# Attention outputs on quarters of the PE array, two tiles a visit, and another order of the opening

## The chip, the cores and the metric

The program runs on one core of a Trainium2 chip. Its engines are PE (TensorE: weight loads and matmuls), ACT (ScalarE), DVE (VectorE), POOL (GpSimd) and SP (SyncE, which issues DMAs here). Each engine takes its own instructions in order and waits on semaphores for the others. The metric is the device time of one execution in microseconds, lower is better.

## What is computed

Three layers follow each other on 4608 tokens of width 512 (8 batches of 576 tokens, 8 heads of 64). The reference, cut:

```python
kv  = einsum('bhsd,bhse->bhde', k, v)            # linear attention, f32
o   = einsum('bhsd,bhde->bhse', q, kv)
rms = sqrt(mean(o * o, axis=-1, keepdims=True) + 1e-06)
x   = (o / rms * g_norm), heads side by side      # (4608, 512)
h   = x @ moe_w_in;  x = (h / (1 + exp(-h))) @ moe_w_out      # d_ff 2048
h   = x @ moe2_w_in; x = (s * relu(h)**2 + b) @ moe2_w_out
```

## The kernel before

**Stages.** The first stage makes seven blocks of 512 tokens of hidden activations with plain products (`emit_h`, 16 groups a block, 112 groups of 12 products `ph`), while the attention of the batches 1 to 7 is worked off between these groups. `hidden1`, `out2`, `hidden3` and `out4` then compute the rest of the two layers with a seven-product scheme for 2x2 blocks. Products of the two layers are three passes over a high and a low part of each operand.

**Attention.** Tokens come in tiles of 128. For a batch, `emit_kv` sums k-transposed times v for the eight heads into one PSUM bank (`pkv`) and copies the eight 64x64 matrices into `kvw`, in which a pair of heads stands as a 128x128 matrix with two blocks on its diagonal and zeros elsewhere; there are two such rooms, for even and odd batches. `emit_qT` transposes a tile of q on PE (`pq`) and copies it on ACT. `emit_out` multiplies it with `kvw`, 4 products of 128x128x128 (`po`); a batch has four tiles and 64 tokens over, and the leftovers of two batches share a fifth tile, with two half products a pair. `emit_squares` and `reduce_sum` give the mean square of each head, `rsqrt_steps` its reciprocal root by twelve DVE operations, `emit_norm` scales the tile (`xnp`), and `emit_xT` transposes it (`px`) and makes the high and low parts `xh` (ACT) and `xl` (DVE) that `ph` reads.

**Order.** The program is in an order written by hand (`manual_schedule`). After each group `ph` of block j, row m, `first_stage` calls `attend(16 * j + m)`. `UNITS` gives for each batch its number of tiles and its first slot; `attend` does what is due at that distance from it: q and kv loads, `emit_kv` two slots ahead, one tile's transposes one slot ahead of its outputs, the root's steps (kept in `between` and run between other DVE work), normalisation, and one tile's `px` a slot. In block 0 `first_stage` also decodes the first layer's weights for later rows: steps `rebias` (ACT), `low`, `sign`, `merge` (DVE), `high` (ACT, the rounded part `wh`), `rest` (DVE, the remainder `wl`).

**Opening.** Batch 0 goes first, alone. Its loads are issued on SP, and on ACT for the leftovers and small columns. `warm_up` keeps PE busy with products that nobody reads. Then come the transposes of q, the kv matrices by pairs of heads, the outputs of the four tiles, squares, root, scaling and `px`; the weights 0 and 1 are decoded beside them.

Of the kernel before, what the change touches and what calls it, by code (L numbers as in the profile page):

```python
# [17 lines left out]
def kernel(  # L18
# [95 lines left out]
    def runs(t):  # L114
        b, c = t
        return [(0, P, b)] if c < TT else [(i * ST, ST, b - 1 + i) for i in range(2)]

# [225 lines left out]
    def emit_kv(b, pairs):  # L343
# [13 lines left out]
        for p, (_, kz, _, vz) in parts:  # L357
            for i, r in enumerate(halves):
                nc.tensor.matmul(ps[r, p, r], kz[i], vz[i], start=False, stop=True, skip_group_check=True)  # L359
        for r in halves:  # L360
            nc.scalar.copy(kvw[b % 2][r, pairs[0]:pairs[-1] + 1, r], ps[r, pairs[0]:pairs[-1] + 1, r])
# [11 lines left out]
    def emit_qT(t):  # L373
        a = q_t.pop(t).rearrange("p h d -> p (h d)")
        ps = ps_a.tile([P, T], F32, tag="a", name=f"pq{t[0]}_{t[1]}")
        for p in range(NP):
            nc.tensor.transpose(ps[:, p * P:(p + 1) * P], a[:, p * P:(p + 1) * P], ident)  # L377
        qT = at_kvw[:, 0].rearrange("p (a t) -> p a t", a=NP)
        nc.scalar.copy(qT.rearrange("p a t -> p (a t)"), ps)
        qT_t[t] = qT  # L380

    def emit_out(t, ps, pairs):

        po = ps.rearrange("p h d -> p (h d)")
# [7 lines left out]
    def emit_squares(t, ps, ms):  # L392

        sq = work.tile([P, H, D], F32, tag="sg", name=f"sq{t[0]}_{t[1]}", bufs=3)
        nc.scalar.activation(sq, ps, AF.Square)
        nc.vector.reduce_sum(ms, sq, axis=AX.X)  # L396

    def rsqrt_steps(r, tiles):
# [10 lines left out]
        for _ in range(3):  # L409
            yield lambda: nc.vector.tensor_mul(a, y, y)  # L410
            yield lambda: nc.vector.scalar_tensor_tensor(a, a, -0.5, ms, op0=ALU.mult, op1=ALU.mult)
            yield lambda: nc.vector.scalar_tensor_tensor(y, a, 1.5, y, op0=ALU.add, op1=ALU.mult)
# [15 lines left out]
    def emit_norm(t, x, y):  # L428
        xn = xn_t.get(t)
        if xn is None:  # L430
            xn = xn_t[t] = xn_page(t)
# [4 lines left out]
    def out_tile(t):  # L436
        b, i = t
        if i == 0:
            r_t[b] = small.tile([P, 4, 6 * H], F32, tag="r", name=f"r{b}", bufs=1)
        ps = ps_a.tile([P, H, D], F32, tag="a", name=f"po{b}_{i}")  # L440
        emit_out(t, ps, range(NP))
        emit_squares(t, ps, r_t[b][:, 0, i * H:(i + 1) * H])
        xn_t[t] = xn_page(t)
        nc.scalar.copy(xn_t[t], ps)
# [98 lines left out]
    def first_qT(t, qs):  # L543
        ps, tag = (ps_a, "a") if t < 2 else (ps_h, "h")
        ps = ps.tile([P, T], F32, tag=tag, name=f"pq{t}")
        for h in range(H):
            r = slice(h % 2 * D, (h % 2 + 1) * D)
            c = slice(h // 2 * P, (h // 2 + 1) * P)
            nc.tensor.matmul(ps[r, c], qs[h // NP][:, h % NP, t, :], ident, start=True, stop=True)
# [3 lines left out]
        nc.scalar.copy(qT, ps)  # L553
# [6 lines left out]
    def attend(slot):  # L560

        for b, n, s in UNITS:
            d = slot - s
            lead = 4 if b == 1 else 8
            if 0 <= d + lead < n:
                load_q(b, d + lead)
            if -1 <= d < NP - 1 and b + 1 < B:
                load_kv(b + 1, d + 1)
        for b, n, s in UNITS:
            d = slot - s  # L570
            if d == -2:
                emit_kv(b, range(NP))
            if 0 <= d < n:
                out_tile((b, d))
            if -1 <= d < n - 1:
                emit_qT((b, d + 1))
# [9 lines left out]
            if TT + 3 <= d < 2 * TT + 3:  # L586
                xT_tile((b, d - TT - 3))
            if n > TT:
                if d == TT + 4:
                    between.extend(rsqrt_steps(r_t[b], [TT]))  # L590
                if TT + 4 <= d < TT + 6:
                    run_between(6)
                if d == TT + 6:
                    norm_tile((b, TT))
                if d == 2 * TT + 3:
                    xT_tile((b, TT))
# [427 lines left out]
    def warm_up(n):  # L1024

        ps = ps_h.tile([P, T], F32, tag="h", name="warm")
        for _ in range(n):
            nc.tensor.matmul(ps, kvw[1][:, 0, :], kvw[1].rearrange("p a t -> p (a t)"), start=True, stop=True)
# [165 lines left out]
    with tc.manual_schedule():  # L1194
# [121 lines left out]
```

## Time and profile before

| | |
|---|---|
| median of 3 runs | 1557.99 us (1557.68 to 1559.7) |
| the profiled execution | 1557.85 us |
| its span, first to last instruction | 1555.7 us |
| busy share of the span | PE 99%, DVE 65%, ACT 53%, POOL 0% |
| granted PE clock, mean | 0.999 |

The rows quoted further down are from this execution, with times from the start of the span. The chain of waits is followed back from the last instruction to what released each; 97% of it is PE. A wait of PE is read from the list of waits; what a stretch costs on PE is read from the start of one piece of the chain to the start of the next. A matmul's record is longer than its slot on the engine, since matmuls overlap; an f32 product leaves two records.

### The profile page before, as it was taken

The page shows a single profiled execution, that of the slowest core. Times are in us where ns is not written, and L with a number is a line of the kernel's source. Part 1 is how long each engine was busy: PE and PEld are TensorE (multiplying, and loading weights), DVE is VectorE, ACT ScalarE, POOL GpSimd, SP SyncE. Part 2 cuts the span into 40 slices and gives each one's busy share as a digit, 9 for nine tenths or more (in the row PEclk, how much of TensorE's full clock was granted, in tenths as well). Part 3 has the DMA queues.
Part 4 walks back from the last instruction along what each step waited for, and adds up shares of the span by engine and source line. Part 5 has one row for each costly group of instructions (what it writes and reads, how often), then busy time and mean ns, then how long its engine had stood idle before and what let it go on. Part 6 is the DMA issues. An engine that isn't in the chain of part 4 may idle for free.

```text
span 1555.7 us, 21812 instructions
## 1 busy us (share of the span) xinstructions
PE 1541.1 (99%) x8184; PEld 1297.8 (83%) x8184; DVE 1017.0 (65%) x1435; ACT 822.4 (53%) x1311; POOL 1.6 (0%) x8
## 2 busy tenths in 40 slices
PE   7999999999999999999999999999999999999999
PEld 5888888888888888888988888888899888888888
DVE  5655466457673968685786666767656767575855
ACT  4655545555465544444545565656555454545554
POOL 0000000000000000000000000000000000000000
PEclk9999999999999999999999999999999999999999
DMA  8988798877665883724669556474577782726242
GB/s 257 302 275 274 265 303 286 293 261 260 254 237 185 349 312 93 242 83 149 217 249 403 210 200 242 176 265 175 200 277 281 292 302 70 243 71 236 87 128 90
DMA packets 228969, 353.77 MB, mean 227 GB/s; under 512 B 56576, under 2 KB 97024, under 8 KB 228864
## 3 DMA queue, kind: packets, MB, share of 16 engines
q1 hardware_dynamic: 163968, 243.83, 46.6%
q10 hardware_dynamic: 64896, 108.55, 18.6%
q8 instruction: 64, 1.05, 0.3%
q14 instruction: 41, 0.34, 0.1%
HBM read 211.81 MB, written 140.51 MB: 226 GB/s over the span
## 4 chain that ended last, share of the span: by engine, by line
PE 97%; DMA 1%; DVE 1%; ACT 0%; issue 0%; SPq 0%; ACTq 0%; DVEq 0%
PE ph L500 19%; PE qy L996 19%; PE qx L996 13%; PE qv L996 13%; PE py L722 12%; PE pv L722 8%; PE px L722 8%; PE po L387 2%; PE px L464 1%; PE pkv L353 1%; PE pt L921 1%; PE pq L377 1%; DMA q<-in_q_dram 1%; DMA kv<-in_v_dram 0%; PE pkv L359 0%; DVE r L396 0%
## 5 line engine op out<-in xcount | busy, mean ns | idle before, releaser
L996 PE MATMUL qy<-o,w 128*128 128x512 f32 (+1 forms) x1440 | 299.1, 368 | 0.0
L996 PEld LDWEIGHTS qy<-o,w 128*128 128x128 f32 x1440 | 251.2, 189 | 45.0
L881 DVE TENSOR_TENSOR o<-ka,o 128x1024 fp32r<-128x1024 f32 (+1 forms) x160 | 178.7, 1117 | 104.8 <-ACT o L879 103.8
L879 ACT CAST o<-ka 128x1024 fp32r<-128x1024 f32 (+1 forms) x160 | 154.6, 968 | 162.9 <-PE qv L996 73.1
L996 PE MATMUL qv<-o,w 128*128 128x512 f32 (+1 forms) x960 | 202.9, 369 | 0.0
L996 PE MATMUL qx<-o,w 128*128 128x512 f32 (+1 forms) x960 | 202.9, 369 | 0.0
L996 PEld LDWEIGHTS qx<-o,w 128*128 128x128 f32 x960 | 167.0, 189 | 29.7 <-DVE o L881 0.2
L996 PEld LDWEIGHTS qv<-o,w 128*128 128x128 f32 x960 | 167.0, 189 | 29.4
L722 PE MATMUL py<-x,w 128*128 128x512 f32 (+1 forms) x720 | 161.2, 368 | 0.0
L722 PEld LDWEIGHTS py<-x,w 128*128 128x128 f32 x720 | 126.5, 189 | 22.7 <-ACT py L777 0.3
L507 ACT ACTIVATE g<-ph 128x512 f32<-128x512 f32 x112 | 67.0, 598 | 145.8 <-PE ph L500 143.5
L500 PE MATMUL ph<-xh,wh 128*128 128x512 f32 x448 | 127.6, 406 | 0.8 <-ACT xh L468 0.8
L879 ACT CAST o<-r 128x1024 fp32r<-128x1024 f32 (+1 forms) x80 | 77.2, 965 | 83.9 <-PE qy L996 43.8
L500 PE MATMUL ph<-xl,wh 128*128 128x512 f32 x448 | 120.4, 390 | 0.0
L500 PE MATMUL ph<-xh,wl 128*128 128x512 f32 x448 | 120.4, 390 | 0.0
L881 DVE TENSOR_TENSOR o<-r,o 128x1024 fp32r<-128x1024 f32 (+1 forms) x80 | 89.4, 1118 | 36.4 <-ACT o L879 35.5
L722 PE MATMUL pv<-x,w 128*128 128x512 f32 (+1 forms) x480 | 111.6, 368 | 0.0
L722 PE MATMUL px<-x,w 128*128 128x512 f32 (+1 forms) x480 | 111.6, 368 | 0.0
L500 PEld LDWEIGHTS ph<-xh,wl 128*128 128x128 f32 x448 | 84.1, 188 | 18.6
L500 PEld LDWEIGHTS ph<-xl,wh 128*128 128x128 f32 x448 | 84.1, 188 | 18.6
L722 PEld LDWEIGHTS px<-x,w 128*128 128x128 f32 x480 | 84.9, 189 | 15.1
L722 PEld LDWEIGHTS pv<-x,w 128*128 128x128 f32 x480 | 84.7, 189 | 14.9
(162 smaller groups left out, 1872.1 us busy)
## 6 DMA issues: line engine op xcount, KB each, us to landing
r<-gt SPq DMA_DIRECT2D x96, 512.0 KB, 4.6
gt<-g ACTq DMA_DIRECT2D x176, 256.0 KB, 2.3
w<-wd SPq DMA_DIRECT2D x84, 512.0 KB, 7.3
gt<-g ACTq DMA_DIRECT2D x56, 512.0 KB, 4.5
wd<-wo SPq DMA_DIRECT2D x112, 256.0 KB, 4.1
wr<-in_moe_w_in_dram SPq DMA_DIRECT2D x16, 1024.0 KB, 6.4
wr<-in_moe_w_out_dram SPq DMA_DIRECT2D x16, 1024.0 KB, 6.5
ka<-gt SPq DMA_DIRECT2D x32, 512.0 KB, 4.0
```

The lines of the kernel that those rows point to most:

```text
L353: nc.tensor.matmul(ps[r, p, r], ka[:, i, d], va[:, i, d], start=(p == pairs[0] and c == 0), stop=False, skip_group_check=True,)
L377: nc.tensor.transpose(ps[:, p * P:(p + 1) * P], a[:, p * P:(p + 1) * P], ident)
L387: nc.tensor.matmul(po[off:off + n, p * P:(p + 1) * P], qT_t[t][:, p, off:off + n], kvw[b % 2][:, p, :], start=True, stop=True,)
L464: nc.tensor.transpose(ps[:, p, :], xn[:, p * P:(p + 1) * P], ident)
L500: nc.tensor.matmul(ps, wt[:, c, :], xt[:, c, :], start=(n == 0 and c == 0), stop=(n == 2 and c == KT - 1))
L507: nc.scalar.activation(both[:, i], ps, AF.Silu)
L722: nc.tensor.matmul(ps, a[s][c], x[t][c], start=(k in (P1, P5) and n == c == 0), stop=(n == 2 and c == 1), skip_group_check=True,)
L879: nc.scalar.copy(o[:, :, 0], x)
L881: nc.vector.tensor_sub(o[:, :, 1], x, o[:, :, 0])
L921: nc.tensor.transpose(ps[:, e * P:(e + 1) * P], self.c[b, h, e][:, r * P:(r + 1) * P], ident)
L996: nc.tensor.matmul(ps, t[:, s], self.o[u][:, i, p], start=(k in (P1, P5) and a == i == m == 0), stop=(a == NA - 1 and i == 1 and m == 2), ...
```

## The change

- `kvw` loses its zeros: for each batch parity, four pairs, two heads on the two halves of the partitions, 64x64 each.
- An output tile is 16 products of 64x64x64. The row half of the array is the head of the pair and picks the PSUM bank, the column half is the half of the tile's tokens. A bank holds the even or the odd heads of two tiles.
- `attend` takes two tiles a visit: transposes of two, outputs of two, then two copies into `xnp` and the squares read from there; `px` of two tiles a visit. The normalisation moves into `norms`, which in block 0 runs ahead of `ph`, in later blocks behind `attend`.
- The root has ten operations with other constants.
- In block 0 `first_weights` decodes one row pair less ahead, and stands before `emit_h`.
- The opening issues q first, then the first weights, k and v, the small columns (now on SP), and the second weights. Its products of q are ordered by halves of the heads, its copies of the kv matrices are on DVE, its squares come in two halves, and the last bank is scaled by eight ACT operations.

The diff, cut:

```diff
-    at_kvw = pair("T", "at_kvw")
-    kvw = [at_kvw[:, 1].rearrange("p (a t) -> p a t", a=NP), const.tile([P, NP, P], F32, tag="kvw1", name="kvw1")]
+    kvw = const.tile([P, 2, NP, D], F32, tag="kvw1", name="kvw")
...
         for r in halves:
-            nc.scalar.copy(kvw[b % 2][r, pairs[0]:pairs[-1] + 1, r], ps[r, pairs[0]:pairs[-1] + 1, r])
+            (nc.scalar.copy if b else nc.vector.tensor_copy)(kvw[r, b % 2, ps_of], ps[r, ps_of, r])
...
+    def emit_qT(b, cs):
+        qT = pair("T", f"qT{b}_{cs[0]}")
+        for n, c in enumerate(cs):
+            a = q_t.pop((b, c)).rearrange("p h d -> p (h d)")
+            ps = bank(f"y{n}_0", f"pq{b}_{c}")
+            for p in range(NP):
+                nc.tensor.transpose(ps[:, p * P:(p + 1) * P], a[:, p * P:(p + 1) * P], ident)
+            nc.scalar.copy(qT[:, n], ps)
...
+    def emit_out(t, banks, pairs):
         for p in pairs:
-            for off, n, b in runs(t):
-                nc.tensor.matmul(
-                    po[off:off + n, p * P:(p + 1) * P], qT_t[t][:, p, off:off + n], kvw[b % 2][:, p, :],
-                    start=True, stop=True,
-                )
+            for i, r in enumerate(ROWS):
+                for c, b in zip(ROWS, sources(t)):
+                    nc.tensor.matmul(
+                        banks[i][c, p, :], qT_t[t][r, p, c], kvw[r, b % 2, p, :], start=True, stop=True
+                    )
...
+    def out_tiles(b, cs):
...
+        for n, c in enumerate(cs):
+            emit_out((b, c), [x[:, n] for x in banks], range(NP))
+            xn_t[b, c] = xn_page((b, c))
...
+        for n in range(2):
+            nc.scalar.copy(x[:, :, :, n], banks[n])
+        for c in cs:
+            emit_squares((b, c), xn_t[b, c], r_t[b][:, 0, c * H:(c + 1) * H])
...
+            if d in (-1, 1, 3):
+                cs = [c for c in (d + 1, d + 2) if c < n]
+                if cs:
+                    emit_qT(b, cs)
+            if d in (0, 2, 4):
+                cs = [c for c in (d, d + 1) if c < n]
+                if cs:
+                    out_tiles(b, cs)
+            if d in (TT + 3, TT + 5):
+                for i in range(2):
+                    xT_tile((b, d - TT - 3 + i))
...
+    def first_weights(m):
+        i = m // 2
+        norms(m)
+        if m % 2 == 0:
+            if i + 1 < NF:
+                decode_first(i + 1, "high", "rest")
+            if i + 2 < NF:
+                decode_first(i + 2, "rebias", "low")
+        elif i + 2 < NF:
+            decode_first(i + 2, "sign", "merge")
+
     def first_stage(j, m, steps):
-        if j == 0:
-            i = m // 2
-            if m % 2 == 0:
-                if i + 2 < NF:
-                    decode_first(i + 2, "high")
-                if i + 3 < NF:
-                    decode_first(i + 3, "rebias", "low")
-            else:
-                if i + 2 < NF:
-                    decode_first(i + 2, "rest")
-                if i + 3 < NF:
-                    decode_first(i + 3, "sign", "merge")
         attend(MT * j + m)
+        if j:
+            norms(MT * j + m)
...
+        qs = [first_load_q(0), first_load_q(1)]
+        kvz = first_load_z()
         load_raw(1, 0, "wr_0")
-        qs = [first_load_q(0), first_load_q(1)]
-        kvs = [first_load_kv(0), first_load_kv(1)]
-        kvz = first_load_z()
+        kvs = [first_load_kv(p) for p in range(NP)]
...
         load_raw(1, 1, "wr_1")
-        kvs += [first_load_kv(2), first_load_kv(3)]
...
         decode_first(0, "rebias", "low", "sign", "merge")
...
+        copy_qT(2)
+        copy_qT(3)
         first_kv(0)
         first_kv(1)
...
+        decode_first(0, "high", "rest")
+        first_out(0)
+        first_kv(2)
+        first_out(1)
+        first_kv(3)
+        first_squares(slice(0, 2))
+        first_out(2)
+        first_out(3)
+        first_squares(slice(2, 4))
+        decode_first(1, "rebias")
...
-        decode_first(1, "rest")
-        decode_first(2, "rebias", "low", "sign", "merge")
+        decode_first(1, "low", "sign", "merge")
...
         for j in range(PB):
             for m in range(MT):
+                if j == 0:
+                    first_weights(m)
                 emit_h(j, m)
                 first_stage(j, m, steps)
```

PE in block 0, from the fourth hidden group's last pass to the first outputs of batch 1. Before:

```order
L500 MATMUL ph_3_542<-xh_402,wl_427 128x512 x4
L377 MATMUL pq_0_570<-ident,qp_66 128x128 x4
L500 MATMUL ph_4_576<-xh_402,wh_451 128x512 x4
L500 MATMUL ph_4_576<-xl_403,wh_451 128x512 x4
L500 MATMUL ph_4_576<-xh_402,wl_470 128x512 x4
L387 MATMUL po_0_603<-kvw_70,at_kvw 128x128 x4
L377 MATMUL pq_1_612<-ident,qp_66 128x128 x4
```

The same place after:

```order
L514 MATMUL ph_3_605<-xh_459,wl_492 128x512 x4
L383 MATMUL pq_0_626<-ident,qp_65 128x128 x4
L383 MATMUL pq_1_632<-ident,qp_65 128x128 x4
L514 MATMUL ph_4_644<-xh_459,wh_532 128x512 x4
L514 MATMUL ph_4_644<-xl_460,wh_532 128x512 x4
L514 MATMUL ph_4_644<-xh_459,wl_534 128x512 x4
L394 MATMUL po_0_0_664<-kvw,qT_0_625 64x64 x2
L394 MATMUL po_0_1_665<-kvw,qT_0_625 64x64 x2
```

The second tile's transposes have moved ahead of the hidden group, and a visit of outputs begins with pairs of 64x64 products (`po_0_0` the even heads' bank, `po_0_1` the odd heads'), sixteen for each of two tiles.

ACT from the last `xh` of batch 0 (the high part of the first block) to the first two Silus `g`. Before:

```order
L468 ACTIVATE xh_402<-px_420,cols 128x4x128
L154 ACTIVATE wr_2_224<-wr_2_224 128x1024
L507 ACTIVATE g_0_449<-ph_0_436 128x512
L173 CAST wh_451<-wf_2_432 128x1024
L154 ACTIVATE wr_3_311<-wr_3_311 128x1024
L507 ACTIVATE g_0_449<-ph_1_456 128x512
```

After:

```order
L482 ACTIVATE xh_459<-px_477,cols 128x4x128
L176 CAST wh_490<-wf_1_486 128x1024
L157 ACTIVATE wr_2_259<-wr_2_259 128x1024
L521 ACTIVATE g_0_509<-ph_0_496 128x512
L521 ACTIVATE g_0_509<-ph_1_517 128x512
```

The rounding of the second weights (`wh` from `wf_1`) stood ahead of all `xh` before; now it stands between the last `xh` and the first Silu.

DVE in the opening, from the first weights' merge (`wf_0`) to the first reduction of squares. Before:

```order
L161 SCALAR_TENSOR_TENSOR wf_0_222<-wr_0_173 128x1024
L176 TENSOR_TENSOR wl_228<-wf_0_222,wh_226 128x1024
L156 TENSOR_SCALAR wr_1_188<-wr_1_188 128x1024
L158 SCALAR_TENSOR_TENSOR wr_1_188<-wr_1_188 128x1024
L161 SCALAR_TENSOR_TENSOR wf_1_309<-wr_1_188 128x1024
L396 TENSOR_REDUCE r_214<-sq_0_362 128x8
```

After:

```order
L164 SCALAR_TENSOR_TENSOR wf_0_257<-wr_0_179 128x1024
L365 COPY kvw<-pkv_0_264 64x64 x2
L365 COPY kvw<-pkv_1_277 64x64 x2
L179 TENSOR_TENSOR wl_292<-wf_0_257,wh_290 128x1024
L365 COPY kvw<-pkv_2_310 64x64 x2
L365 COPY kvw<-pkv_3_339 64x64 x2
L1263 TENSOR_REDUCE r_210<-sq_0_352 128x2x2
```

The copies of the kv matrices have come to DVE between the first weights' steps, and the second weights' decoding has gone to behind `xl`.

## Rows read from the trace of the kernel before

**Rows 1.** The page's busy times by engine, with shares of the span.

```profile
PE 1541.1 (99%) x8184; PEld 1297.8 (83%) x8184; DVE 1017.0 (65%) x1435; ACT 822.4 (53%) x1311; POOL 1.6 (0%) x8
```

**Rows 2.** PE's waits from 40 to 430: total us, times, longest.

```profile
PE px L464 <- DVE xnp L432: 0.7, 1, 0.7
```

**Rows 3.** Timeline, 0 to 45: start, us, engine, line, operation, count, [idle before, releaser].

```profile
1.77 6.31 PE L1028 MATMUL warm<-kvw 128*128 128x512 f32 x8 [1.77 <-POOL kvw L1205]
...
7.80 1.10 ACT L154 ACTIVATE wr<-wr 128x1024 f32<-128x1024 f32 x1 [4.08 <-DMA kvz<-in_k_dram]
...
10.82 3.28 PE L549 MATMUL pq<-ident,q 128*64 128x128 f32 x56 [1.06 <-DMA q<-in_q_dram]
...
14.93 0.43 ACT L361 COPY at_kvw<-pkv 64x64 f32<-64x64 f32 x2 [0.20 <-PE pkv L359]
...
19.71 0.69 PE L353 MATMUL pkv<-kv 128*64 128x64 f32 x16 [0.65 <-DMA kv<-in_v_dram]
...
24.27 2.06 ACT L395 ACTIVATE sq<-po 128x512 f32<-128x512 f32 x4 [0.58 <-PE po L387]
...
24.90 2.46 DVE L396 TENSOR_REDUCE r<-sq 128x8 f32<-128x512 f32 x4 [3.00 <-ACT sq L395]
...
30.15 2.48 DVE L432 TENSOR_TENSOR xnp<-po,r 128x512 f32<-128x512 f32 x4
...
30.90 3.63 PE L464 MATMUL px<-ident,xnp 128*128 128x128 f32 x16 [2.56 <-DVE xnp L432]
32.03 0.69 ACT L468 ACTIVATE xh<-px,cols 128x512 fp32r<-128x512 f32 x1 [4.76 <-PE px L464]
32.75 3.28 DVE L469 SCALAR_TENSOR_TENSOR xl<-px,cols,xh 128x512 fp32r<-128x512 f32 x4
...
37.08 0.69 DVE L156 TENSOR_SCALAR wr<-wr 128x1024 int32<-128x1024 int32 x1
...
37.88 1.23 DVE L158 SCALAR_TENSOR_TENSOR wr<-wr 128x1024 int32<-128x1024 int32 x1
...
38.35 0.60 ACT L507 ACTIVATE g<-ph 128x512 f32<-128x512 f32 x1 [2.08 <-PE ph L500]
...
40.40 1.06 ACT L173 CAST wh<-wf 128x1024 fp32r<-128x1024 f32 x1 [1.45 <-DVE wf L161]
```

**Rows 4.** The chain of waits in the first stage: start, us, what, records.

```profile
35.30 8.45 PE ph L500 x36
...
49.38 0.44 PE pq L377 x4
...
52.58 0.89 PE po L387 x8
...
83.44 2.77 PE ph L500 x12
...
112.28 10.90 PE ph L500 x48
...
150.03 1.02 PE po L387 x16
151.05 8.39 PE ph L500 x36
```

**Rows 5.** Timeline of PE, 40 to 125: products on halves of the array, records.

```profile
43.69 2.09 PE L353 MATMUL pkv<-kv 128*64 128x64 f32 x64
45.70 0.68 PE L359 MATMUL pkv<-kvz 64*64 64x64 f32 x16
...
69.69 0.27 PE L387 MATMUL po<-at_kvw 128*64 128x128 f32 x1
69.70 0.27 PE L387 MATMUL po<-kvw,at_kvw 128*64 128x128 f32 x1
69.80 0.27 PE L387 MATMUL po<-at_kvw 128*64 128x128 f32 x1
```

**Rows 6.** Busy by stretch: us, PE, PEld, DVE, ACT, POOL, granted clock, DMA, GB/s.

```profile
30.90:34.40 3.50, 3.50 (x16) 3.25 (x16) 3.24 (x5) 2.05 (x3) 0.00 (x0) 0.51 0.93 327
```

More of the change, by code (lines that the diff above doesn't have):

```diff
@@ L408, in rsqrt_steps @@
         )
[L409 to L412, printed above, removed]
+        yield lambda: nc.vector.tensor_mul(a, y, y)
+        yield lambda: nc.vector.tensor_mul(a, a, ms)
+        yield lambda: nc.vector.scalar_tensor_tensor(a, a, -10.0 / 3.0, a, op0=ALU.add, op1=ALU.mult)
+        yield lambda: nc.vector.scalar_tensor_tensor(y, a, 5.0, y, op0=ALU.add, op1=ALU.mult)
+        yield lambda: nc.vector.tensor_mul(a, y, y)
+        yield lambda: nc.vector.scalar_tensor_tensor(a, a, -0.0263671875, ms, op0=ALU.mult, op1=ALU.mult)
+        yield lambda: nc.vector.scalar_tensor_tensor(y, a, 0.5625, y, op0=ALU.add, op1=ALU.mult)
     between = []
@@ L428, in emit_norm @@
     def emit_norm(t, x, y):
-        xn = xn_t.get(t)
-        if xn is None:
-            xn = xn_t[t] = xn_page(t)
+        xn = xn_t[t]
         nc.vector.tensor_tensor(xn, x, y.rearrange("p (h o) -> p h o", o=1).to_broadcast([P, H, D]), op=ALU.mult)
     r_t = {}
-    def out_tile(t):
-        b, i = t
-        if i == 0:
+    def out_tiles(b, cs):
+        if cs[0] == 0:
             r_t[b] = small.tile([P, 4, 6 * H], F32, tag="r", name=f"r{b}", bufs=1)
[L440 to L444, printed above, removed]
+        k = len(cs)
+        banks = [bank(f"a_{n}", f"po{b}_{cs[0]}_{n}").rearrange("p (t a d) -> p t a d", t=2, a=NP)[:, :k] for n in range(2)]
+        for n, c in enumerate(cs):
+            emit_out((b, c), [x[:, n] for x in banks], range(NP))
+            xn_t[b, c] = xn_page((b, c))
+        if k == 2:
+            x = xn_pages[cs[0] // 2].rearrange("p t (a i d) -> p t a i d", a=NP, i=2)
+        else:
+            x = xn_t[b, cs[0]].rearrange("p (o a i) d -> p o a i d", o=1, i=2)
+        for n in range(2):
+            nc.scalar.copy(x[:, :, :, n], banks[n])
+        for c in cs:
+            emit_squares((b, c), xn_t[b, c], r_t[b][:, 0, c * H:(c + 1) * H])
     def norm_tile(t):
@@ L541, in first_load_q, with first_qT, copy_qT @@
         return a
[L543 to L546, printed above, removed]
+    def first_qT(t, half, qs):
+        if half == 0:
+            ps, tag = (ps_a, "a") if t < 2 else (ps_h, "h")
+            first["pq", t] = ps.tile([P, T], F32, tag=tag, name=f"pq{t}")
+        ps = first["pq", t]
+        for h in range(half * NP, (half + 1) * NP):
             r = slice(h % 2 * D, (h % 2 + 1) * D)
             c = slice(h // 2 * P, (h // 2 + 1) * P)
-            nc.tensor.matmul(ps[r, c], qs[h // NP][:, h % NP, t, :], ident, start=True, stop=True)
+            nc.tensor.matmul(ps[r, c], qs[half][:, h % NP, t, :], ident, start=True, stop=True)
+    def copy_qT(t):
         if t % 2 == 0:
@@ L552, in first_qT @@
         qT = first["qT"][:, t % 2 * T:(t % 2 + 1) * T]
-        nc.scalar.copy(qT, ps)
+        nc.scalar.copy(qT, first["pq", t])
         qT_t[0, t] = qT.rearrange("p (a t) -> p a t", a=NP)
@@ L558, with norms @@
     UNITS = [(1, 5, 4), (2, 4, 16), (3, 5, 25), (4, 4, 36), (5, 5, 52), (6, 4, 68), (7, 5, 84)]
-    def attend(slot):
+    def norms(slot):
         for b, n, s in UNITS:
             d = slot - s
[L564 to L576, printed above, removed]
             if d == TT - 1:
@@ L591, in attend @@
                 if TT + 4 <= d < TT + 6:
-                    run_between(6)
+                    run_between(5)
                 if d == TT + 6:
                     norm_tile((b, TT))
-                if d == 2 * TT + 3:
-                    xT_tile((b, TT))
+    def attend(slot):
+        for b, n, s in UNITS:
+            d = slot - s
+            lead = 6 if b == 1 else 8
+            if 0 <= d + lead < n:
+                load_q(b, d + lead)
+            if -1 <= d < NP - 1 and b + 1 < B:
+                load_kv(b + 1, d + 1)
+        for b, n, s in UNITS:
+            d = slot - s
+            if d == -2:
+                emit_kv(b, range(NP))
+            if d in (-1, 1, 3):
[9 more added lines that the diff above has]
+                    xT_tile((b, d - TT - 3 + i))
+            if n > TT and d == 2 * TT + 3:
+                xT_tile((b, TT))
     RING = ("xh_1", "xl_1", "xh_0", "xl_0")
```

86 lines of the change are left out of this document (47 added, 39 removed).

## The prediction

> **What bounds the kernel now.** First the page's busy times: TensorE (PE) is busy 99% of the span [rows 1]. The time therefore falls only where PE gets less to do or stops waiting. Second, what PE waited for after the opening: one wait of 0.7 us, for the normalised tile `xnp` [rows 2]. Third, the timeline of the opening [rows 3]: the first hidden product starts only at 35.30 [rows 4], and everything before it is a chain across PE, ACT and DVE, so there an order of work counts as much as an amount. Fourth, the chain of waits in the first stage (112 groups of hidden products `ph`, with attention visits between them) is PE's own work, one thing behind the other [rows 4]; a visit made shorter there shortens the kernel by as much. After that stage the diff touches nothing, and I cost it at nothing.
>
> **Part 1: the output products `po`.** Before, a tile takes four 128x128x128 f32 products, which are eight records in 0.89 us [rows 4]; there are 28 such tiles behind the opening: 24.9 us. The four tiles made of two batches' tails take 1.02 each, and the hidden products behind run 8.39 instead of 3/4 of 10.90 = 8.18, which is 0.21 of switching [rows 4]: 4 x 1.23 = 4.9. Together 29.8 us of PE.
>
> After, a tile is sixteen products of 64x64x64, each on a quarter of the array. Rows of before show halves, not quarters. There two products on the two column halves start within 0.01 us of each other [rows 5], and a run of 64 records of 64 columns costs (2.09 - 0.69) / 48 = 0.0292 us a record [rows 3, 5]; the 64-row form is as fast, 0.68 for 16 records where the full height takes 0.69 [rows 3, 5]. A pair of records thus takes 0.058 us, a product (two records) 0.117, with two products beside each other. Whether the upper and the lower row half also run beside each other no row shows. From below: they do, and four products take 0.117; two tiles (32 products) are 8 x 0.117 = 0.93. From above: they don't, and two tiles are 1.87. I take the lower value: the two row halves read different partitions and write different banks, which is one thing less to share than the column halves have, and those overlap fully. The Trainium skill ("TensorE: Matmul & The Clock Gate", "Part 3: Packing small matmuls — row/col tiling") reports a speed-up of 3.07 with four row strips beside each other; by it the lower value holds, and no run here shows it.
>
> Each visit changes the array's division twice. The tail visits price that: 1.23 - 16/2 x 0.109 = 0.36, with 0.109 for a pair of 128-column records (the next pair of the run in rows 5 starts that much later). Fourteen visits of two tiles: 14 x (0.93 + 0.36) = 18.1. Four of one tail tile: 4 x (0.47 + 0.36) = 3.3. Sum 21.4, so **-8.4 us**. The switch could cost as little as the 0.045 that a `px` visit shows (2.77 against 10.90 / 4 [rows 4]), which is 18 x 0.32 = 5.7 us better, or 0.2 more a visit, 3.6 worse.
>
> **Part 2: fewer visits.** `pq` (0.44 for four transposes [rows 4]) and `px` keep their number of transposes but come two tiles a visit. Per unit of work about 5 visits fall away, over seven units 35, of which a few shared a slot: some 28 x 0.045 = **-1.3 us**. The ACT work per pair of tiles is the same (two copies of the transposes, two copies and two squares of the output, all near 0.6). The squares now read the copy in SBUF behind it, and PE needs neither soon: the banks of `po` are used again two slots later, over 6 us, against 2.4 us of ACT.
>
> **Part 3: the 0.7 us wait.** In the first block the normalisation steps now stand ahead of the hidden product, not behind it, the tiles' squares end two slots earlier, and the reciprocal root has ten steps, not twelve. From the end of the tail tile's visit, ACT needs some 1.3 us, then DVE 0.62 for the reduction, 2 x 1.23 for weights, six root steps of 0.23 and 2 x 0.62 for the first `xnp` pair: 7.0 us, and PE comes for it after three groups of 2.73, 8.2 us. The wait goes, **-0.7 us**, and what is late next is PE itself.
>
> **Part 4: the opening.** Loads: q stands first, the weights behind it. By 10.8 both had landed before too (the second q released PE then [rows 3]); the bytes ahead of that point are the same, so the weights now land near 10.8. The k and v loads no longer have a megabyte of weights in their midst; between 10.8 and 19.6 before, 2.6 MB landed, 0.30 MB/us, so the last of them (2.1 MB behind 10.8) lands by 17.8. Worked along the engines, with durations of rows 3:
> PE: warm-up from 1.3 (one memset to wait for, not two), 6.31 long, to 7.6; transposes of q 64 x 3.28/56 = 3.75, to 11.3. They wait for no load any more.
> ACT: two copies (0.6 each) end at 11.0, the weights' first step takes 1.1, to 12.1. DVE: two steps of 1.23, to 14.6, and behind these the copies of the first two key-value matrices, 0.43 each as on ACT, to 15.5. These copies are DVE's now, queued behind the weights, and PE waits for them; that is the price of the move.
> Then output products, two more key-value products of about 1.1 each, and DVE's subtraction for the weights' low part (1.23) beside them: last outputs at 19.9. Squares are split in two halves of four; the first half lies beside products, the second half ends on ACT at 21.5 (four of 0.4; of full size one is 2.06/4) and on DVE at 21.9 (a last reduction of half of 2.46/4). Root: twelve steps took the 2.79 from 27.36, where the reductions ended, to 30.15; ten are 2.3, to 24.2. Three products of 0.62 on DVE and the fourth bank on ACT: the first page is whole at 25.4, the second at 26.1.
> Transposes `px`: at full clock 4 x 0.44, at half clock 3.63, as before, when PE had done nothing in the 2.6 us ahead and had 0.51 of the clock granted, the 1.2 GHz level [rows 6]. Now 1.8 us lie idle; I take full clock. ACT's four `xh` of 0.69 start at 25.9 and set the end: first hidden product at 28.7 (29.6 at half clock) against 35.30.
>
> **But this is not all kept.** DVE finishes `xl` at 29.9 (four of 0.82 behind `xh`), and only then decodes the second weights: 0.7 + 1.23 + 1.23, to 33.1. ACT now has the rounding of these weights (1.06) and the next ones' first step (1.1) queued *ahead* of the first Silu; before, that rounding was done ahead of `xh`, and only the first step stood between. So that Silu (0.60) is done at 33.1 + 1.06 + 1.1 + 0.6 = 35.9. PE's third group of hidden products needs the bank that this Silu empties: it starts at 36.0 and not at 28.7 + 5.6 = 34.3. Before, it started at 35.30 + 2/3 x 8.45 = 40.9 [rows 4]. The opening gives **-4.9 us**, with a wait of some 1.6 us of PE on the Silu. Bounds: -6.6 if that wait isn't there, 0 if loads or DVE's order eat it all.
>
> **Sum.** The profiled execution took 1557.85 us (2.15 of it outside the span), the median is 1557.99: the same. 1557.85 - 8.4 - 1.3 - 0.7 - 4.9 = **1542.5 us**.
>
> **Rivals.**
> *A: row halves don't overlap.* One record per 0.0292 us is then the most that PE starts. Every two-tile visit costs 0.93 more, a tail visit 0.47: 14 x 0.93 + 4 x 0.47 = 14.9 back, 1557.4 us, no change that can be measured. For it: no row shows more. Against it: within a pair the starts are 0.01 apart, so issuing isn't the limit at 0.0292.
> *B: a mean rate in between.* The same mechanism with a ceiling between 0.0146 (four products beside each other) and 0.0292 us a record; halfway, 0.0219, is 1.40 a visit of two tiles, +7.5 in all, 1550.0. By the Trainium skill ("TensorE: Matmul & The Clock Gate", "Wait — 56ns, not 53.3ns?") starts never come closer than about 25 ns: as a mean that would be 1.6 a visit and, as an estimate, 1553.2; start by start the rows of pairs contradict it.
> *C: slower.* Between row halves PE drains, as it does when the array's division changes. There are 14 x 16 + 4 x 8 = 256 such changes. Without overlap (1557.4) 0.015 us each already makes it slower by over 0.2%; at 0.18, half of the 0.36 of a visit, it is 46 us, 1603. Against it: the column halves change without any gap.
> *D: the opening gives nothing.* DVE's queue (kv copies behind the weights) or a late load holds PE until 35 as before: 1547.4.
>
> **How the numbers follow.** Forecast 0.72 (part 1 as taken, opening -3 to -6.6), D 0.09, B 0.08, A 0.07, C 0.04. A measurement tells 0.2%, 3.1 us, from no change. Faster: forecast, D, B: 0.88, less 0.02 for mixtures: 0.86. Same: A and the mixtures, 0.09. Slower: C and A with a wait on top, 0.05. Range: below, the cheap switch, 1542.5 - 5.7 = 1536.8, less a microsecond for the opening; above, B nearly to its end, 0.026 us a record (+11.7). It holds forecast, D and most of B; A and C are left out. 1536 to 1554.
>
> **What would show it.** Right: `po` groups of 64 records near 0.93 + some switching, no PE wait on `xnp` in the first block, first `ph` near 28.7, and a PE wait of 1 to 2 us on the Silu before the third group. Wrong in part 1: 64 records in 1.9. Wrong in part 4: `px` later than 27, with DVE or a DMA as its releaser. It would all be wrong if PE showed new waits after the first block, on ACT above all, whose visits now come in lumps.

## The result, and the profile after

The changed kernel takes **1541.56 us** (median of 4, 1541.25 to 1541.69), beside 1557.84 of the kernel before in the same comparison (4 runs, 1557.63 to 1559.7): ratio 0.989, 95% interval 0.9878 to 0.9902, 16.3 us less. The profiled executions differ by as much: spans 1555.7 and 1539.8, 15.9 less. The ledger below is worked out between these two.

The page's busy times after (cf. [rows 1]): PE is busy 13.4 us less, and still sets the time.

```profile
PE 1527.7 (99%) x9016; PEld 1281.8 (83%) x9016; DVE 1011.3 (66%) x1422; ACT 823.9 (54%) x1319; POOL 1.2 (0%) x7
```

What PE waits for after, over the whole span, the largest (total us, times, longest). Of the first block's wait on `xnp` [rows 2] nothing is left; the first line here belongs to the opening. New are the wait on the Silu's `g`, which was forecast, and two that were not: the one on `r`, and one of the two on `py` (before, PE waited for `py` once, 0.3 us):

```profile
PE px L478 <- DVE xnp L1301: 1.6, 1, 1.6
...
PE ph L514 <- ACT xh L482: 1.2, 1, 1.2
PE po L394 <- DVE kvw L365: 1.1, 1, 1.1
PE ph L514 <- ACT g L521: 0.9, 1, 0.9
PE po L394 <- DVE r L1263: 0.9, 1, 0.9
PE py L750 <- ACT py L805: 0.8, 2, 0.5
```

The timeline of the opening after (start, us, engine, line, operation, count, idle before), beside [rows 3]:

```profile
7.27 3.71 PE L565 MATMUL pq<-ident,q 128*64 128x128 f32 x64
...
18.70 1.40 PE L394 MATMUL po<-kvw,qT 64*64 64x64 f32 x60 [0.90 <-DVE r L1263]
18.76 0.38 ACT L1262 ACTIVATE sq<-po 128x256 f32<-128x256 f32 x1 [1.20 <-DVE r L1263]
...
25.33 1.97 PE L478 MATMUL px<-ident,xnp 128*128 128x128 f32 x16 [1.59 <-DVE xnp L1301]
26.03 2.42 ACT L482 ACTIVATE xh<-px,cols 128x512 fp32r<-128x512 f32 x4 [0.36 <-PE px L478]
26.75 2.73 DVE L483 SCALAR_TENSOR_TENSOR xl<-px,cols,xh 128x512 fp32r<-128x512 f32 x4 [0.87 <-ACT xh L482]
28.50 1.20 PE L514 MATMUL ph<-xh,wh 128*128 128x512 f32 x4 [1.20 <-ACT xh L482]
32.63 1.05 ACT L176 CAST wh<-wf 128x1024 fp32r<-128x1024 f32 x1 [4.18 <-DVE wf L164]
33.59 1.14 ACT L157 ACTIVATE wr<-wr 128x1024 f32<-128x1024 f32 x1
34.63 1.06 ACT L521 ACTIVATE g<-ph 128x512 f32<-128x512 f32 x2
35.26 1.20 PE L514 MATMUL ph<-xh,wh 128*128 128x512 f32 x4 [0.91 <-ACT g L521]
```

The first hidden product starts at 28.50 (35.30 before), the third group, behind the Silu, at 35.26 (40.88 before). The last six lines are the chain that the prediction drew: `xl` ends at 29.48, DVE decodes, ACT rounds (`wh`) and starts the next weights (`wr`) ahead of the Silu, and PE waits 0.91.

The chain of waits in the first stage after (start, us, what, records), beside [rows 4]; two tiles now stand in one visit:

```profile
47.50 1.09 PE po L394 x64
48.59 2.95 PE ph L514 x12
51.54 0.87 PE pq L383 x8
52.42 2.73 PE ph L514 x12
...
62.41 0.62 PE po L394 x32
63.03 8.39 PE ph L514 x36
```

PE's records in the timeline at the same places, for the rate of the quarters:

```profile
47.43 1.16 PE L394 MATMUL po<-kvw,qT 64*64 64x64 f32 x64
...
62.34 0.69 PE L394 MATMUL po<-kvw,qT 64*64 64x64 f32 x32
```

32 records more take 1.16 - 0.69 = 0.47 us, 0.0147 a record: half of the 0.0292 of two products beside each other. Four run beside each other.

### The profile page after: what moved, and what is told of

Read it like the earlier page. It is cut to its first block, busy times and chain, and to the rows that moved or that the text cites. A ratio compares the mean times of both kernels' runs of the same rounds, so it can differ in the third digit from the quotient of the medians.

```text
span 1539.8 us, 23455 instructions
## 1 busy us (share of the span) xinstructions
PE 1527.7 (99%) x9016; PEld 1281.8 (83%) x9016; DVE 1011.3 (66%) x1422; ACT 823.9 (54%) x1319; POOL 1.2 (0%) x7
## 3 DMA queue, kind: packets, MB, share of 16 engines
q8 instruction: 71, 1.16, 0.3%
## 4 chain that ended last, share of the span: by engine, by line
PE 98%; DVE 1%; ACT 1%; issue 0%; DMA 0%; SPq 0%; ACTq 0%; POOL 0%; POOLq 0%
PE ph L514 20%; PE qy L1024 19%; PE qx L1024 13%; PE qv L1024 13%; PE py L750 12%; PE pv L750 8%; PE px L750 8%; PE po L394 1%; PE pkv L356 1%; PE px L478 1%; PE pt L949 1%; PE pq L383 1%; PE warm L1057 0%; PE pkv L362 0%; DMA kv<-in_v_dram 0%
```

## The experiments

Each experiment's kernel but the last four is the changed one with at most an edit or two; the diffs are against it (of the last four against experiments 4 and 3), and all compute the whole result. The kernel before took 1559.71 us beside the first four, 1558.79 beside the four after these, 1557.83 and 1558.74 beside the last two pairs, and 1557.84 beside the result: so a difference between an experiment's time and 1541.56 is between two comparisons (by the ratios, those of the first four are 0.3 to 0.7 us smaller), and the shares are better read from the profiled executions.

**1. Is it the order through the quarters that lets the row halves overlap?** The four pairs of heads of one row half, then those of the other; the same products.

```diff
-        for p in pairs:
-            for i, r in enumerate(ROWS):
+        for i, r in enumerate(ROWS):
+            for p in pairs:
```

> The changed kernel with the output products in another order: all products on the upper row half of the array first, then all on the lower, instead of going through the four quarters in turn. Same products, same result. My theory: the gain of part 1 is that four quarters run beside each other, and products start in the order written, so with this order only the two column halves overlap: a two-tile visit goes from 1.09 us of records to about 2.0, a tail visit from 0.62 to 1.1, and the time from 1541.6 to 1556 (14 x 0.93 + 4 x 0.47 = 14.9). Rival: the engine looks far enough ahead to start the lower half's products anyway, or the gain lay in the dropped zeros alone: 1541.6 to 1543.

Measured 1549.13 us (1548.52 to 1549.54), ratio 0.9934 (0.992 to 0.9949): between the two. The visit of two tiles in PE's timeline of this kernel:

```profile
48.02 1.56 PE L394 MATMUL po<-kvw,qT 64*64 64x64 f32 x64
...
63.80 0.98 PE L394 MATMUL po<-kvw,qT 64*64 64x64 f32 x32
```

A visit is 0.40 longer, a tail's 0.29: 14 x 0.40 + 4 x 0.29 = 6.8; the opening lost 0.6 more (third group at 35.85; behind a wait of 1.58 ahead of the last outputs the granted clock was 0.50 from 19 to 21, and experiment 5 shows that this comes without any edit too), and the wait of 0.5 on `py` isn't there. Together 6.9, beside 7.1 between the spans of the profiled executions (1546.9 and 1539.8). The direction is the theory's: the four quarters overlap fully only if they are named in turn. Its size was wrong, and the rival holds in part. Records of one quarter start 0.0585 apart. A tail's two runs have eight such starts each, eight in all if the row halves overlap and sixteen if they don't; 0.29 more is five more, thirteen, so three starts at the seam run beside the next run. A visit has three seams, 32 - 9 = 23 starts, seven more than in turn: 0.41. The trace of the tail's visit shows the same in single records: the first pair of the second run starts at 64.096, 0.17 ahead of the last record of the first run (64.265, the one that signals its bank). So PE doesn't start these products strictly in the order written, but it looks ahead by less than half of such a run.

**2. One tile a visit again**, quarters kept, the normalisation behind `ph` as before:

```diff
-            if d in (0, 2, 4):
-                cs = [c for c in (d, d + 1) if c < n]
-                if cs:
-                    out_tiles(b, cs)
...
+            if 0 <= d < n:
+                out_tiles(b, [d])
...
-        norms(m)
...
-        if j:
-            norms(MT * j + m)
+        norms(MT * j + m)
```

> The changed kernel with one tile a visit (transposes, outputs and px), the normalisation in block 0 again behind the hidden group. My theory: every visit of outputs pays 0.36 us for two changes of the array's division, so 14 more visits cost 5.0, the px and pq visits 0.5 to 1.3, the xnp wait up to 0.7: 1547.5 to 1548.6. Rival: the change of division hides behind other work and two tiles a visit bring nothing: 1541.6 to 1542.5.

Measured 1547.43 us (1547.31 to 1547.85), ratio 0.9924 (0.991 to 0.9939): 5.9 back, at the lower end of what the theory had. Its waits show the one on `xnp` again (L439, behind `ph` in the first block), and the chain shows what a visit of one tile costs:

```profile
PE px L478 <- DVE xnp L439: 1.1, 1, 1.1
```

```profile
92.42 0.63 PE po L394 x32
93.05 0.58 PE pq L383 x4
93.63 2.76 PE ph L514 x12
```

The stage, from the third group to the end of the last, takes 376.95, 6.16 more than after. The wait is 1.1 of it. `pq` takes 0.58 here and 0.44 elsewhere, the group behind it 2.76 and not 2.73, so a tile costs 0.80 and two cost 1.60, where a visit of two costs 1.31 (1.09 and 0.22 of the group behind it): 14 x 0.29 = 4.1. The last 1.0 is left for the visits of `pq` and `px`, which came back too. Twice the visits pay nearly twice for switching the array's division: it belongs to the visit, not to the products.

**3. The old order of loads**, the new order of work:

```diff
+        load_raw(1, 0, "wr_0")
         qs = [first_load_q(0), first_load_q(1)]
+        kvs = [first_load_kv(0), first_load_kv(1)]
         kvz = first_load_z()
-        load_raw(1, 0, "wr_0")
-        kvs = [first_load_kv(p) for p in range(NP)]
+        load_raw(1, 1, "wr_1")
+        kvs += [first_load_kv(2), first_load_kv(3)]
```

> The changed kernel with the opening's loads in the order of before: first weights, q, k and v of two pairs, leftovers, second weights, the other k and v; all else as changed. My theory: the last k and v land near 21 instead of under 18, the last output products come 3 us later, and so do px and the first hidden product (about 31.5 instead of 28.5): 1544 to 1545. Rival: DVE's queue sets the opening, the loads wait there anyway, and the order of loads is worth less than 1 us: 1541.6 to 1542.5.

Measured 1545.45 us (1545.0 to 1546.32), ratio 0.9913 (0.9896 to 0.9929), 3.9 back. The first hidden product starts at 31.94, 3.4 later. Its timeline, and a row by stretch (start:end, us, PE, PEld, DVE, ACT, POOL, granted clock, DMA, GB/s):

```profile
9.29 3.71 PE L565 MATMUL pq<-ident,q 128*64 128x128 f32 x64 [1.64 <-DMA q<-in_q_dram]
...
16.54 1.34 PE L394 MATMUL po<-kvw,qT 64*64 64x64 f32 x32 [1.94 <-DVE kvw L365]
```

```profile
16.50:20.00 3.50, 3.46 (x84) 3.16 (x84) 2.34 (x6) 1.13 (x2) 0.00 (x0) 0.55 0.98 292
```

So q is late by 2.0, and then something that nobody had forecast: PE waited 1.94, and behind that the granted clock was 0.55, near the 1.2 GHz level, over 3.5 us full of work. Experiments 9 to 12 take that up.

**4. The old order of products, copies and squares** with the new loads: weights ahead of q's copies, kv copies on ACT, squares behind all outputs, weights decoded behind `ph`. The core of the diff:

```diff
-        for half in range(2):
-            for t in range(TT):
+        decode_first(0, "rebias", "low", "sign", "merge")
+        decode_first(0, "high", "rest")
+        for t in range(TT):
+            for half in range(2):
                 first_qT(t, half, qs)
...
+            copy_qT(t)
...
-            (nc.scalar.copy if b else nc.vector.tensor_copy)(kvw[r, b % 2, ps_of], ps[r, ps_of, r])
+            nc.scalar.copy(kvw[r, b % 2, ps_of], ps[r, ps_of, r])
```

> The changed kernel with the new loads but the opening's products, copies and squares in the order of before, the kv copies on ACT, and the weights decoded as far ahead as before (behind the hidden group). My theory: products, copies and squares in the new order are worth some 2.5 of the 5.7 us that the third hidden group comes earlier, and the loads the other 3: 1543.5 to 1545, without the wait for the first Silu (0.9) but with the first hidden product near 31.5 to 32.5. Rival one: the order of products carries it all: 1547. Rival two: it carries nothing, and the loads do it all: 1541.

Measured 1550.13 us (1549.15 to 1550.73), ratio 0.9941 (0.9926 to 0.9955): worse than each of the three had it. The first hidden product comes at 35.46, no earlier than before the change, though the loads are the new ones. Its timeline and its clock:

```profile
14.52 2.04 ACT L571 COPY qT<-pq 128x512 f32<-128x512 f32 x4
15.15 1.12 PE L356 MATMUL pkv<-kv 128*64 128x64 f32 x16 [4.85 <-DMA cols<-in_g_norm_dram]
```

```profile
15.10:26.10 11.00, 10.34 (x209) 9.03 (x209) 3.92 (x4) 4.82 (x14) 0.00 (x0) 0.50 0.69 242
```

q's copies stand on ACT behind the rounding of weights that, with q loaded first, now land later. The key-value product needs a bank which the first of these copies empties (it starts 0.6 behind the copies' start; the DMA that the row names has long been issued), and PE idles 4.85. Then the clock is 0.50 over the next 11 us. Behind the opening PE waits 2.7 us (2.1 for `xnp` at L439, 0.7 before the change, and 0.6 for `g`).

**5. The changed kernel itself on the second chip**, to compare the next three with:

> The changed kernel once more, unaltered, beside the next three on one chip: some 16 us below the kernel before on the same chip.

1541.57 us (1541.02 to 1542.33), ratio 0.9887 (0.9871 to 0.9904). The first hidden product is at 28.89, the third group at 35.65: the opening varies by 0.4 from one execution to another. In this one PE waited 1.44 us ahead of the last outputs, and behind that the granted clock was near the 1.2 GHz level:

```profile
18.80:20.80 2.00, 1.93 (x61) 1.84 (x61) 0.64 (x3) 0.58 (x3) 0.00 (x0) 0.55 1.12 355
```

So the changed kernel itself doesn't always keep the full clock in its opening.

**6. The Silu ahead of the third weights' first step**, to take the wait of 0.91 away:

```diff
-            if i + 2 < NF:
+            if m and i + 2 < NF:
                 decode_first(i + 2, "rebias", "low")
...
                 emit_h(j, m)
+                if j == m == 0:
+                    decode_first(2, "rebias", "low")
```

> The changed kernel with one step moved: the third weights' first step (rebias on ACT, low on DVE) issued behind the first hidden group, so that the first Silu no longer stands behind it on ACT. My theory: the 0.9 us that PE waits for this Silu before the third hidden group goes, and nothing else is late: 0.9 us less than the changed kernel. Rival: the second weights' rounding (1.05 on ACT) or the third weights' later decoding holds PE instead: no difference.

1541.75 us (1540.41 to 1543.53), ratio 0.989 (0.9875 to 0.9905): no difference that can be told. The wait is gone (the third group starts 5.73 behind the first, not 6.76), but the profile has two new ones of the same kind, 1.6 us in all, ending at 72.6 and 106.7:

```profile
PE ph L514 <- ACT g L521: 1.6, 2, 0.9
```

ACT's timeline there: a DMA that ACT had to issue waited for the load of q, and behind it two copies and two squares came in one lump, ahead of a Silu.

```profile
102.59 1.08 ACT L456 COPY xnp<-po 128x512 f32<-128x512 f32 x2 [2.68 <-DMA qp<-in_q_dram]
```

Experiment 8 has the same moved step and neither wait, so the step alone doesn't bring them; this profile is also of the longest of the four executions (1543.53).

**7. A room of its own for the fourth square**, which waits for a reduction after (`sq` at 18.76 above):

```diff
-                sq = work.tile([P, 2, NP, D], F32, tag="sg", name=f"sq0_{n}", bufs=3)
+                if n < TT - 1:
+                    sq = work.tile([P, 2, NP, D], F32, tag="sg", name=f"sq0_{n}", bufs=3)
+                else:
+                    sq = room("v_0", [P, 2, NP, D], F32, f"sq0_{n}")
```

> The changed kernel with a room of its own for the fourth square of each half in the opening, which now waits for the first square's reduction on DVE, behind two kv copies, and holds PE's last output products (two waits, 0.9 and 0.2 us). My theory: the last output products end 0.7 to 1.1 us earlier, and so does the first hidden product: 0.6 to 1.1 us less than the changed kernel. Rival: DVE's own chain (kv copies, then eight reductions) is the limit: under 0.3 us.

1541.22 us (1540.81 to 1542.02), ratio 0.9887 (0.9872 to 0.9901). PE's wait of 0.90 on `r` is gone, but PE waits 1.8 for `xnp` instead of 1.6, and the first hidden product comes at 28.28: 0.2 to 0.6 earlier. DVE's reductions now follow each other without a gap, and its chain sets the end, as the rival had it. But this opening's first outputs started at 15.02, 0.5 later than after; from there to `px` it took 10.1 us, where it took 10.8 after. So the edit shortens that part, as the theory had it, and 0.35 less than in experiment 5 isn't resolved in the time.

**8. Both edits together**:

> Both of these edits together. If they lie on one path behind each other: 1.5 to 2.0 us less than the changed kernel. If the Silu's wait only moves when the opening ends earlier (DVE's decoding starts behind xl, which comes earlier too): the same sum. Rival: one of them hides the other, 0.9.

1540.69 us (1539.55 to 1542.24), ratio 0.9883 (0.9869 to 0.9898). The third group starts at 34.02 and no wait on `g` is left, but 0.9 less than experiment 5 on the same chip, the rival's number, isn't resolved: the ranges overlap. It is the fastest version seen, and not shown to be faster.

**9 and 10. Is it the clock?** Experiments 4 and 3 with PE's idle stretch to be filled by products that nobody reads (five in the old opening, two with the old loads):

```diff
+        warm_up(5)
```

> The old order of the opening with the new loads, as in the run without this edit (1550.1 us, first hidden product at 35.46, third hidden group at 41.15), and in addition five products that nobody reads, put on PE behind the transposes of q, where PE idled 4.85 us. In that run the granted clock was 0.50 from 15.0 to 27.0, the 1.2 GHz level, and a run of 16 key-value records took 1.12 us where the changed kernel shows 0.69. Theory: the idle stretch brought the clock down, and much of what the old order seemed to cost was the clock. Then the granted clock is 1.00 in 15 to 27, 16 records take 0.69, PE's work from 15.2 to the last output ends at about 22 and not at 26, the first hidden product starts at 31 to 32 and the time is 1545.5 to 1547. Rival: the chain over ACT (weights, copies of q, copies of the key-value matrices) sets the end whatever PE's clock; the first hidden product stays behind 34.5 and the time is 1549 to 1550. What the old order still costs then, against 1541.6, is order alone.

> The old order of loads with the new order of work, as in the run without this edit (1545.45 us, first hidden product at 31.94), and in addition two products that nobody reads, put on PE behind the second key-value product, where PE idled 1.94 us. In that run the granted clock was 0.55 from 16.5 to 20.0. Theory: about 1.4 us of the 3.4 us by which the first hidden product came later was the clock, the rest the late loads: the granted clock stays 1.00, the first hidden product starts at about 30.5 and the time is 1544.0 (1543.5 to 1544.5). Rival: the late loads account for all of it, as DVE's chain follows the weights and not PE: first hidden product at 31.9, 1545.4.

1556.62 us (1555.89 to 1558.12), ratio 0.9992 (0.9982 to 1.0001), and 1547.64 us (1547.19 to 1548.02), ratio 0.993 (0.9913 to 0.9946): both slower than without. The filling didn't fill. It needed what the real work waited for, a bank with q in it in the one, the key-value matrices in the other, so it ran *behind* the gap, ahead of the real work. In experiment 9:

```profile
16.11 6.26 PE L1057 MATMUL warm<-kvw 128*128 128x512 f32 x10 [5.05 <-ACT qT L571]
...
22.30 0.69 PE L356 MATMUL pkv<-kv 128*64 128x64 f32 x16
```

One thing it did show: from 22.2 on the clock was full, over the very products of experiment 4's half-clock row.

```profile
22.20:29.60 7.40, 6.79 (x210) 5.76 (x210) 2.45 (x2) 3.16 (x10) 0.00 (x0) 1.00 0.05 8
```

The same work (210 records, there 209) takes 7.4 us in place of 11.0. The half clock cost 3.6 us there.

**11 and 12. Filled with products that wait for nothing** (the identity with itself, into the still empty bank of the last output; 20 in the old opening, 8 with the old loads):

```diff
+        def fill(n):
+            for _ in range(n):
+                nc.tensor.matmul(pss[TT - 1][:, 0, :2], ident, ident, start=True, stop=True)
...
+        fill(20)
```

> The old order of the opening with the new loads again (1550.1 us, first hidden product at 35.46), with PE's idle stretch of 4.85 us behind the transposes of q filled: this time by 20 products of the identity with itself, into the bank of the last output, which is empty there, so that they wait for nothing (the unread products of the run before this one needed a bank that ACT still had to empty, waited through the whole stretch and ran behind it). Theory: the idle stretch brings the clock to 0.50 for the 12 us behind it, and that costs 3.7 us (from the first key-value product to the last output 10.9 us at 0.50, 7.2 at 1.00 in the run before this one). Then the clock stays at 1.00, 16 key-value records take 0.69, the first hidden product starts at 31.5 to 32 and the time is 1546 to 1547. Rival: ACT's and DVE's chain sets the end at either clock: first hidden product behind 34.5, 1549 to 1550. A third case: the clock falls all the same, and nothing changes.

> The old order of loads with the new order of work again (1545.45 us, first hidden product at 31.94, granted clock 0.55 from 16.5 to 20.0), with PE's idle 1.94 us ahead of the first outputs filled by eight products of the identity with itself into the empty bank of the last output. Theory: the clock stays at 1.00 and some 1.4 us of the 3.4 us by which the first hidden product came later go: first hidden product at about 30.5, 1544.0 (1543.5 to 1544.5). Rival: the late loads account for all of it, as DVE's chain follows the weights: 31.9, 1545.4.

The old loads: 1543.44 us (1543.33 to 1543.55), ratio 0.9903 (0.9886 to 0.9919). The same stretch as in experiment 3:

```profile
16.50:20.00 3.50, 3.21 (x115) 2.84 (x118) 2.29 (x6) 1.80 (x4) 0.00 (x0) 1.00 0.96 275
```

Full clock, and the first hidden product at 30.86, 1.1 earlier than in experiment 3 with nothing else changed. So of the 3.4 by which the old loads delay it, 1.1 is the clock and 2.3 the late data: the theory's split (1.4 and 2.0), a little off.

The old opening: 1548.43 us (1547.92 to 1550.09), ratio 0.9937 (0.9922 to 0.9952); first hidden product at 33.42, 2.0 earlier than in experiment 4, where 3.5 to 4 were expected and the rival had less than 1: between the two. The products stay at full clock up to the next wait and lose it there:

```profile
20.44 0.91 PE L394 MATMUL po<-kvw,qT 64*64 64x64 f32 x32 [1.37 <-ACT kvw L365]
```

```profile
15.10:20.40 5.30, 3.92 (x124) 3.42 (x124) 1.67 (x3) 3.52 (x9) 0.00 (x0) 1.00 0.95 366
20.40:24.00 3.60, 3.25 (x85) 2.78 (x85) 2.25 (x2) 1.15 (x5) 0.00 (x0) 0.71 0.08 15
```

On ACT the kv copy stands behind the first step of the second weights, whose load lands at 19.0. What the old order still costs against the new one, 33.42 - 28.50 = 4.9, holds the order and the rest of a lower clock; the two weren't separated.

When the first hidden product and the third group start, in us from the span's start, by one profile each (the first row's kernel has the old output products too):

| loads | order of work | first | third |
|---|---|---|---|
| old | old (before) | 35.30 | 40.88 |
| new | old | 35.46 | 41.15 |
| new | old, gap filled | 33.42 | 39.10 |
| old | new | 31.94 | 38.71 |
| old | new, gap filled | 30.86 | 37.63 |
| new | new (after) | 28.50 | 35.26 |

The new loads alone bring nothing, the new order alone 3.4, both 6.8. With the gaps filled the loads alone bring 1.9 and the order alone 4.4, 6.3 together: by these rows most of what the two lack when apart was the clock.

## Why the prediction was right

1542.5 was forecast, 1541.56 came. Term by term, between the profiled executions:

| term | forecast | measured |
|---|---|---|
| output products and switching | -8.4 | -8.6 |
| fewer visits of `pq` and `px` | -1.3 | -1.6 |
| wait on `xnp` in block 0 | -0.7 | -0.7 |
| opening | -4.9 | -5.6 |
| behind the first stage | 0 | +0.6 |
| sum | -15.3 | -15.9 |

The opening's miss of 0.7 and the 0.6 behind the first stage nearly cancel: that the sum came so close is in part luck.

**Part 1** held as worked. Four quarters overlap: 0.0147 a record, where the lower bound was 0.0146. A visit of two tiles is 1.09, and the hidden group behind it 2.95 where one without a switch takes 2.73, 1.31 in all (1.29 forecast); a tail's is 0.62 + 8.39 - 8.18 = 0.83 (0.83). 14 x 1.31 + 4 x 0.83 = 21.7 (21.4). Before, the 28 tiles and the tails took 30.3 and not 29.8, since two of the 28 take 1.15, which I left out. Experiments 1 and 2 show both halves of this: the order through the quarters is worth 7, the pairing of tiles 5, of which 4 are on the outputs. This refutes rivals A, B and C: no ceiling above 0.0147, no drain between row halves. The Trainium skill ("TensorE: Matmul & The Clock Gate", "Wait — 56ns, not 53.3ns?") keeps starts some 25 ns apart; this trace doesn't bear that out for products on different quarters, whose mean distance is 14.7 ns over 32 records. The Trainium skill's "Part 3: Packing small matmuls — row/col tiling" on the same page has row strips run beside each other; this trace agrees, with 0.0147 a record on four quarters.

**Part 2.** Behind a visit of two transposed tiles a hidden group takes 2.73, what it takes without any visit, so nothing is left of the 0.045; the term came out at 1.6, as the rest of the stage's -10.9 (from the third group to the end of the last, 381.69 before and 370.79 after).

**Part 3** held: no wait on `xnp` in the first block.

**Part 4** held in its chain: 28.7 forecast, 28.50 measured; D (35) falls. `px` ran at full clock, 1.97 for the sixteen where [rows 3] have 3.63. The term that was mis-sized is `xl`: 0.82 each was read from a row of before in which DVE waited between them for `xh`, and ACT for `px` at half clock; without that, four take 2.73, 0.68 each. `xl` so ended at 29.48 and not 29.9, the rest of the chain followed, and PE's wait on the Silu was 0.91, not 1.6. The fourth square's wait for its room (above) was not foreseen; it didn't show in the sum, as the transposes began 0.3 earlier than worked out (7.27, not 7.6), and the last outputs ended at 20.1, not 19.9.

"I cost it at nothing", of all **behind the first stage**, missed 0.6, of which 0.46 is a wait of PE at 982, which has no counterpart in the profile before. ACT's timeline after, just ahead of it:

```profile
978.76 1.71 ACTq L763 DMA_DIRECT2D gt<-g  x1
980.52 1.05 ACT L698 CAST x<-x 128x1024 fp32r<-128x1024 f32 x1 [1.59 <-issue]
```

The same store took 0.39 to issue before (at 995.41). Between the profiles its issue takes from 0.39 to 1.73, and PE's wait there follows it: 0.46 with 1.71, 0.48 with 1.73 (experiment 5), 0.34 with 1.59 (experiment 3), 0.43 with 1.68 (experiment 7), 0.23 with 1.48 (experiment 4), always the issue less 1.25, and none at 1.18 or less (experiment 1). So the wait is that store's, and it comes and goes. Why its issue is held up wasn't tried.

The chances have a slip: forecast, D and B add to 0.89, not to 0.88.

**What the prediction didn't see** is why the new order and the new loads had to come together. It summed the opening along the engines at full clock and had the clock in mind only for `px`. An order that leaves PE idle in the middle of the opening can also lose the clock for the work behind. The 28.50 is of an execution that kept the full clock; the other profile of the same kernel didn't, and started at 28.89.

## What to carry to other kernels

Work that multiplies half of the array with zeros can be cut into quarters, if neighbours in the program name different quarters in turn, and if several such pieces share a visit, for the switch of the division costs over a third of the visit's work (1.31 - 0.94 = 0.37, beside 0.94). A chain over four engines is worth writing down instruction by instruction: the sum came out within 0.2 us at the first product. Durations for it should come from rows in which the engine waited for nothing between its instructions; and PE's idle stretches in it can cost twice, as time and as clock.

## What the hardware showed that I had not expected

- A wait of 4.85 us was followed by 11 us at 0.50 of the clock, one of 1.94 by 3.5 us at 0.55, one of 1.37 by 3.6 us at 0.71, although PE was at least 90% busy in each; [rows 6] are the same in the kernel before, behind 2.56. Behind 1.44 in the changed kernel itself (experiment 5) it was 0.55. The length of the wait alone doesn't decide it: behind 1.12 after it stayed at 1.00 (rows below), and so it did behind waits of 1.69 in experiment 6, 1.62 in experiment 7 and 2.05 in experiment 8 (the sixteen `px` behind it took 1.96, and 3.63 at half clock [rows 3]). What else decides it these runs don't show. Filling the 1.94 kept it at 1.00. The same 210 records: 7.4 us at 1.00, 11.0 at 0.50.
- Unread products meant to keep PE busy take the waits of their operands and banks with them: in experiment 9 they ran for 6.26 us, behind the gap.
- Products on quarters overlap fully when four neighbours name four different quarters, 1.16 us for 64 records, and only at the seams when they come by row halves, 1.56. There PE started a run's first pair 0.17 us ahead of the last record of the run before.
- The issue of a DMA from ACT can hold that engine for 1.71 us (978.76 after; 0.39 for the same store before). In experiment 6 one that waited for an earlier load to land left ACT idle for 2.68 us (up to 102.59).

Rows of the comparison, by stretch: the changed kernel, and experiment 6 behind its wait of 1.69, over as long a stretch as in experiment 3 above:

```profile
14.50:20.10 5.60, 4.64 (x169) 4.00 (x169) 4.19 (x12) 2.50 (x6) 0.00 (x0) 1.00 1.06 389
14.90:18.40 3.50, 3.28 (x108) 2.81 (x108) 2.56 (x7) 1.89 (x4) 0.00 (x0) 1.00 1.04 391
```
